# A fixed order for the ELU steps, weight casts, x operands and output copies between the first and the second chunk of an attention and feed-forward kernel

## The chip, the cores and the metric

The kernel runs on one core of a Trainium2 chip. Its time is that of one execution on the device, in microseconds (us), and the figure of a kernel is the median of its runs. A profile is one more execution, recorded by the hardware profiler; positions in it are us from the start of its span. PE is TensorE's matmul, DVE is VectorE, ACT is ScalarE, POOL is GpSimd, SP is the queue that issues the transfers.

## The reference

Attention over 8 sequences of 576 tokens with 8 heads of 64 is followed by a feed-forward block with an ELU; both in float32. Four heads see a window of 32 keys, four see every fourth key of a window of 128:

```python
scores = scale * np.matmul(q, k.transpose(0, 1, 3, 2))
scores = np.where(masks[None, :, :, :], scores, -1000000000.0)
attn = np.exp(scores - np.max(scores, axis=-1, keepdims=True))
attn = attn / (np.sum(attn, axis=-1, keepdims=True) + 1e-09)
x = np.matmul(attn, v)            # then [B, S, H * D] as 4608 rows of 512
h = x @ w_in                      # 512 -> 2048
g = np.where(h > 0.0, h, np.exp(np.minimum(h, 0.0)) - 1.0)
return g @ w_out                  # 2048 -> 512
```

## The kernel before, in words

**Chunks and tiles.** The feed-forward block goes over nine chunks of 512 tokens (`c`), and in a chunk over 16 tiles of 128 hidden features (`f`). Tile `f` of chunk `c` is `gemm1(c, f)`: `x` times a block of `w_in`, into one bank of PSUM, `h0` or `h1`. In chunk 0 the banks alternate; from chunk 1 on the tiles all use `h0`, and `h1` is lent to the attention. Then come the ELU steps, and two tiles later (`LAG = 2`, kept by the list `pend` and by `flush`) `second_product`: four groups of three matmuls that add the tile's share to the output banks `o_ps`. "Tile 14's product" below is this second product of `f = 14` in chunk 0.

**Split operands.** A matmul in full precision is made of three: every operand is cast to a high part (ACT, `copy` into a rounded type) and a rest (DVE, `tensor_tensor` subtract). `split_w` (lines 180 and 181) makes both for two blocks of 128x512 weights at once: `split_w(15, ...)` makes those of the second products of tiles 14 and 15, and `split_late(0)` those of the first products of tiles 0 and 1, used from chunk 1 on (in chunk 0 these tiles went in full precision). `split_late(0)` writes to the room `r3`, which held raw words of weights until their conversion (lines 137 to 149, DVE). `split_x(c)` (lines 521 and 522) makes `xh` and `xl` of the chunk's `x` for four pairs of heads; chunk 1 takes 64 tokens of sequence 0 and 448 of sequence 1, so it is 8 casts on ACT and 8 rests on DVE. There is one buffer for each of `xh` and `xl`, so they can be written only when the last tile of the chunk before has read them. The first product of a tile is 12 matmuls: for each pair of heads the high weights by `xh` and by `xl`, then the rest of the weights by the four `xh`.

**ELU steps of a tile** (`elu`): exp (line 550) and relu (552) on ACT, `max(h, 0) - e` on DVE (557), the cast `gh` on ACT (563) and the rest `gl` on DVE (564). The DVE step at line 557 is the last reader of the PSUM bank in chunk 0. In chunk 1, ACT first copies the bank to SBUF (548), and lines 559 and 560 stand for relu and the DVE step.

**Attention beside it.** While chunk 0 runs, `second_attention` makes `x` of sequence 1, one step for each tile: scores (E), probabilities with six transposes on DVE at line 405 (X), outputs (O) for four pairs of heads. The X step of the last pair is at `f = 12`, O of the third pair at `f = 14` and O of the last at `f = 15`. An O step is products on PE into `a_ps` and two copies on ACT (line 286 or 289) into `x32`, from which `split_x(1)` reads. At the first tile of chunk 1 a piece of scores for sequence 2 follows tile 14's product; it uses both `a_ps` banks and `h1`.

**What sets the order.** PE's instructions stay in the order in which they are written (`mm` marks each with `inorder`). On the other engines a planner orders the instructions by a simulated time line and the order of writing; `tc.issue_after(ins)` adds that what follows on the engine of `ins` comes behind it, and `inorder` (`keep_in_program_order`) pins an instruction behind the one written just before it on its engine. `vec` and `act` (lines 412 to 420) are DVE and ACT with every instruction pinned so; before, they are used in the last tiles of chunk 2 and in the chunks from 3 on. Each engine's queue runs in order, so an instruction that waits holds all behind it.

At the border the kernel before has these lines:

```python
        if c == 1:
            with tc.issue_after(hidden[-4]), tc.issue_after(below[-4]):
                last_x = split_x(c)
...
            while c == 1 and split < min(12, f + 2):
                with tc.issue_after(last_transpose[1] if split < 2 else last_x[0]), tc.issue_after(low[NF - 3 - F2] if split < 2 else last_x[1]):
                    with tc.issue_after(low[-1]), tc.issue_after(high[-1]):
                        split_late(split)
```

so `split_late(0)` is behind `gh` and `gl` of tile 15.

Of the kernel before, what the change touches and what calls it, by code (L numbers as in the profile page):

```python
# [66 lines left out]
def body(ctx: ExitStack, tc: tile.TileContext, q, k, v, masks, w_in, w_out, out):  # L67
# [105 lines left out]
        o = k % 2 * 2  # L173
        return slots(f"r{1 + (k - 12) // 2}", o, o + 4), slots(f"r{1 + (k - 12) // 2}", o + 1, o + 5)

    def split_w(k, t0, t1, places=None):

        h, l = places or places_of(k, t0, t1)
        w = full2[k][:, t0:t1, :]
        nc.scalar.copy(out=h, in_=w)  # L180
        nc.vector.tensor_tensor(out=l, in0=w, in1=h.bitcast(F32), op=ALU.subtract)
        for t in range(t0, t1):
            wh[need[2 * k + t]], wl[need[2 * k + t]] = h[:, t - t0, :], l[:, t - t0, :]

    LATE = {0: (("r3", 0, 1), ("r3", 2, 3)), 1: (("r3", 4, 5), ("r3", 6, 7)), 2: (("a7", 0, 1), ("a7", 2, 3)),
# [107 lines left out]
    def outputs(b, hp, places, vt, tr, keep=lambda ins: ins):  # L293
        products(places, vt, tr)
        return copies(b, hp, places, keep)
# [10 lines left out]
    def banks():  # L306

        return [ps_a.tile([P, TC], F32, name=f"a_ps{i}") for i in range(2)]
# [199 lines left out]

    masked, maxima = [], []

    def split_x(c):
        for hp in range(NC):
            xh[hp] = xp.tile([P, TC], F32R, name=f"xh{hp}")
            xl[hp] = xp.tile([P, TC], F32R, name=f"xl{hp}")
            t0 = c * TC
            while t0 < (c + 1) * TC:
                b, o = divmod(t0, S)
                n = min(S - o, (c + 1) * TC - t0)
                u = slice(t0 - c * TC, t0 - c * TC + n)
                src = x32[b][:, hp, o:o + n]  # L520
                last_cast = nc.scalar.copy(out=xh[hp][:, u], in_=src)
                last = nc.vector.tensor_tensor(out=xl[hp][:, u], in0=src, in1=xh[hp][:, u].bitcast(F32), op=ALU.subtract)
                t0 += n
        return last.ins, last_cast.ins

# [13 lines left out]
    def gemm1(c, f):  # L539
        for h_ps in first if (c, f) == (0, 0) else product1(c, f):  # L540
            pass
        return h_ps

    def elu(h_ps, c, f, v=nc.vector, a=nc.scalar):
        e = fp.tile([P, TC], F32, name="e")
        if 0 < c < B - 1:
            h = fp.tile([P, TC], F32, name="h", bufs=2)
            a.copy(out=h, in_=h_ps)
            h_ps = h
        a.activation(out=e, in_=h_ps, func=AF.Exp)  # L550
        if c == 0:
            below.append(nc.scalar.activation(out=e, in_=e, func=AF.Relu, scale=-1.0, bias=1.0).ins)
            if f < F2:
                g = fp.tile([P, TC], F32, name="gh", bufs=3)
                hidden.append(nc.vector.scalar_tensor_tensor(out=g, in0=h_ps, scalar=0.0, in1=e, op0=ALU.max, op1=ALU.subtract).ins)
                return g, None
            hidden.append(nc.vector.scalar_tensor_tensor(out=e, in0=h_ps, scalar=0.0, in1=e, op0=ALU.max, op1=ALU.subtract).ins)
        else:
            a.activation(out=e, in_=e, func=AF.Relu, scale=-1.0, bias=1.0)
            v.scalar_tensor_tensor(out=e, in0=h_ps, scalar=0.0, in1=e, op0=ALU.max, op1=ALU.subtract)  # L560
        gh = slots("r3", 4)[:, 0, :] if (c, f) == (CS - 1, NF - 1) else fp.tile([P, TC], F32R, name="gh", bufs=3)
        gl = slots("r3", 6)[:, 0, :] if (c, f) == (CS - 1, NF - 2) else slots("a7", 0)[:, 0, :] if (c, f) == (CS - 1, NF - 1) else fp.tile([P, TC], F32R, name="gl", bufs=2)
        high.append(a.copy(out=gh, in_=e).ins)
        low.append(v.tensor_tensor(out=gl, in0=e, in1=gh.bitcast(F32), op=ALU.subtract).ins)
        return gh, gl

    def store(c, t, o_ps):
        o = fp.tile([P, DM], F32, name="e")
# [189 lines left out]
    def second_attention():  # L758

        x32[1] = xp.tile([P, NPAIR, S], F32, name="x32", bufs=2)  # L760
        state = [None] * NPAIR

        for step in " E0 X0 E1 X1 O0  E2 X2 O1  E3 X3  O2 O3".split(" "):
            if step:
                what, hp = step[0], int(step[1])
                i = NPAIR + hp
                if what == "E":
                    s_ps = banks()
                    scores(s_ps, *qk_of.pop(i), True)
                    state[hp] = exponentials(1, hp, [[(0, NU, a)] for a in s_ps])  # L770
                    load_qk(i + 1)
                    if hp == 0:
                        load_v(i + 1)
                    if hp == NPAIR - 1:
                        load_qk(i + 2)
                elif what == "X":
                    state[hp] = probabilities(*state[hp])
                else:
                    b, _, tr = state[hp]
                    outputs(b, hp, [(a, i * NA, (i + 1) * NA) for i, a in enumerate(banks())], v_of.pop(NPAIR + hp), tr)  # L780
                    load_v(i + 2)
            yield

    rooms = [room(0, hp) for hp in range(NPAIR)]

# [36 lines left out]
    split = 0  # L822
    pend = []
    made = {}

    def flush(n):
        while len(pend) > n:
# [4 lines left out]
    att = second_attention()  # L832
    for c in range(CS):
        if c == 1:
            with tc.issue_after(hidden[-4]), tc.issue_after(below[-4]):
                last_x = split_x(c)

        elif c > 1:
            split_x(c)
        if c == 1:  # L840
            for j in (14, 15, 12, 13, *range(12)):
                keep_whole(j)
        when = WHEN.get(c, ())
        for f in range(NF):
            while c == 0 and ready < min(NF, f + AHEAD):
                for j in (ready, ready + 1):
                    with tc.issue_after(below[-1] if below else last_copy.ins):
                        magnitude(j)
                if f > 0:
                    with tc.issue_after(last_conversion.ins):  # L850
                        last_conversion = convert(ready // 2, behind=maxima[-1] if maxima else None)
                for j in (ready, ready + 1):
                    if j + 2 * NR < NF:
                        load_w(j + 2 * NR)
                ready += 2
            if c == 0 and f == F1 - 2:
                with tc.issue_after(masked[-1]), tc.issue_after(below[-1]):
                    split_x(0)
# [3 lines that stand above are left out]
                        split_late(split)  # L862
                split += 1
            strict = (vec, act) if c == CS - 1 and f >= LAST else ()
            pend.append((c, f, elu(gemm1(c, f), c, f, *strict)))
            if c == 1:
                keep_plain(f)
            if (c, f) == (0, 0):

                for part in slice(0, 2 * DM), slice(2 * DM, 4 * DM):  # L870
                    with tc.issue_after(last_conversion.ins), tc.issue_after(hidden[-1]):
                        last_conversion = convert(1, part=part)
            if c == 0 and F1 <= f + 2 <= NF:

                with tc.issue_after(hidden[-2]):
                    split_w(f + 1, 0, 2 if f >= F2 else 1)
            if c == 0:
                with tc.issue_after(hidden[-1] if f > 1 else last_step[NPAIR - 1]):
                    next(att)
            flush(LAG if c < CS - 1 or f < NF - 2 else LAG + f - (NF - 3))  # L880
            if (c, f) in COMBINE:
                with tc.issue_after(low[-1]), tc.issue_after(high[-1]):
                    combine(COMBINE[c, f])
            if (c, f) == (CS - 1, NF - 2):
                made[0] = scores_piece(CS + 1, (0, 1))
            if f in when:
                i = when.index(f)
                if i % 2 == 0:
                    made[i] = scores_piece(c + 1, (i, i + 1))
                else:  # L890
                    outputs_piece(made.pop(i - 1))
            if (c, f) == (CS - 1, OPER):
                take_places()
                moving["temporary"], late = [halved(slots("a5", o)) for o in range(2)], moving["temporary"]
                for what in sum(OPERANDS[:7], []):
                    moving_operand(CS, what, vec, act)
# [73 lines left out]
```

## Time and profile before

| | |
|---|---|
| median of 3 runs | 894.13 us (890.94 to 895.24) |
| the profiled execution | 892.59 us, its span 890.7 us |
| mean granted clock of TensorE | 0.990 |
| PE busy | 866.9 us, 97% |
| DVE busy | 610.1 us, 68% |
| ACT busy | 458.6 us, 51% |
| POOL busy | 6.0 us, 1% |
| DMA | 170.68 MB, mean 192 GB/s |

The span is from the first to the last recorded instruction; the profiled execution's time has 1.9 us more around it. A row of a time line gives the start, the time from the first start to the last end of the instructions merged in it, engine, line, operation, output and inputs by the program's names, and in square brackets the idle time of the engine before it and what ended that. Matmuls overlap, so the time from one start to the next is what one costs. PEclk is the clock that the throttle granted to TensorE, as a share of the full one.

### The profile page before, as it was taken

How to read it: one execution, taken by the hardware profiler on the slowest of the kernel's cores; microseconds unless marked ns; L12 is line 12 of the kernel's file. 1: busy time of each engine (PE TensorE's matmuls, PEld its weight loads, DVE VectorE, ACT ScalarE, POOL GpSimd, SP SyncE). 2: the span in 40 equal slices, each digit the busy share in tenths (PEclk: the TensorE clock that was granted, in tenths of full speed). 3: DMA queues.
4: the chain of work that ended last, by engine and by line, in shares of the span. 5: the costliest groups of instructions: out<-in, count | busy, mean ns of one | idle time of the engine just before them, and what ended most of it. 6: DMA issues, size and time to landing. Idle time of an engine off the chain costs nothing. (4 is left out here: it accounts for less than half of the span.)

```text
span 890.7 us, 17847 instructions
## 1 busy us (share of the span) xinstructions
PE 866.9 (97%) x7424; PEld 728.4 (82%) x7424; DVE 610.1 (68%) x921; ACT 458.6 (51%) x783; POOL 6.0 (1%) x12
## 2 busy tenths in 40 slices
PE   6999998999989999999999999999999999999998
PEld 4545676887878888898989998989899999998996
DVE  6999996958578878874977487748775533353332
ACT  3665665745655564544554454545554453454334
POOL 2000000000000000000000000000000000000000
PEclk8999998999999999999999999999999999999999
DMA  9996334321463556867576577666765566567541
GB/s 345 380 353 244 118 102 142 109 91 67 160 223 114 192 176 197 255 191 222 179 252 212 182 221 226 220 199 221 212 186 160 175 206 186 171 182 221 185 142 48
DMA packets 66961, 170.68 MB, mean 192 GB/s; under 512 B 6752, under 2 KB 21440, under 8 KB 66880
## 3 DMA queue, kind: packets, MB, share of 16 engines
q1 hardware_dynamic: 66880, 169.54, 59.2%
q8 instruction: 59, 0.97, 0.4%
q14 instruction: 22, 0.18, 0.1%
HBM read 141.20 MB, written 28.31 MB: 190 GB/s over the span
## 5 line engine op out<-in xcount | busy, mean ns | idle before, releaser
L104 PE MATMUL h<-xh,r 128*128 128x256 f32 (+1 forms) x984 | 225.3, 311 | 8.3 <-ACT r L180 3.7
L104 PEld LDWEIGHTS h<-xh,r 128*128 128x128 f32 x984 | 166.2, 192 | 19.9 <-ACT r L180 4.2
L104 PE MATMUL h<-xl,r 128*128 128x256 f32 (+1 forms) x492 | 143.6, 309 | 0.6 <-DVE xl L418 0.6
L104 PE MATMUL o_ps<-a,r 128*128 128x512 f32 x480 | 117.0, 391 | 0.0
L418 DVE SCALAR_TENSOR_TENSOR a-1_3251<-a-1_3251,a 128x1024 f32<-128x1024 f32 x48 | 58.7, 1223 | 83.2 <-ACT a L418 83.0
L418 DVE TENSOR_TENSOR a-1_3251<-h,e 128x512 f32<-128x512 f32 x72 | 49.7, 690 | 82.5 <-PE h L104 82.1
L104 PEld LDWEIGHTS h<-xl,r 128*128 128x128 f32 x492 | 94.4, 192 | 10.4 <-issue 3.5
L104 PEld LDWEIGHTS o_ps<-a,r 128*128 128x128 f32 x480 | 87.6, 188 | 16.5
L104 PE MATMUL o_ps<-a,gh 128*128 128x512 f32 x248 | 89.3, 463 | 0.0
L418 ACT COPY e<-h 128x512 f32<-128x512 f32 x72 | 42.2, 586 | 79.2 <-PE h L104 64.8
L104 PE MATMUL h<-a,r 128*128 128x256 f32 x576 | 77.5, 284 | 0.0
L104 PEld LDWEIGHTS h<-a,r 128*128 128x128 f32 x576 | 74.0, 191 | 3.0
L418 ACT COPY a-1_3251<-h 128x512 f32<-128x512 f32 x24 | 14.1, 587 | 109.6 <-PE h L104 109.6
L104 PEld LDWEIGHTS o_ps<-a,gh 128*128 128x128 f32 x248 | 46.3, 188 | 24.2 <-issue 17.2
L418 ACT ACTIVATE a<-a 128x1024 f32<-128x1024 f32 (+1 forms) x56 | 57.0, 1030 | 1.3
L104 PE MATMUL o_ps<-r,r 128*128 128x512 f32 x212 | 56.8, 391 | 0.0
L104 PE MATMUL o_ps<-a,a 128*128 128x512 f32 x216 | 54.6, 391 | 0.0
L418 ACT ACTIVATE a<-a-1_3251 128x1024 f32<-128x1024 f32 x48 | 51.0, 1062 | 1.3 <-DVE a-1_3251 L418 0.5
L104 PEld LDWEIGHTS o_ps<-a,a 128*128 128x128 f32 x216 | 39.4, 189 | 7.4
L418 ACT CAST r<-a-1_3251 128x1024 fp32r<-128x1024 f32 x32 | 33.6, 1051 | 22.2 <-DVE a-1_3251 L418 22.1
L104 PEld LDWEIGHTS o_ps<-r,r 128*128 128x128 f32 x212 | 38.7, 188 | 7.3
L418 DVE TENSOR_TENSOR r<-a-1_3251,r 128x1024 fp32r<-128x1024 f32 x32 | 39.0, 1218 | 6.6 <-ACT r L418 6.1
(176 smaller groups left out, 1434.0 us busy)
## 6 DMA issues: line engine op xcount, KB each, us to landing
r<-combined SPq DMA_DIRECT2D x168, 512.0 KB, 4.1
vt<-v SPq DMA_DIRECT2D x30, 384.0 KB, 4.3
kt<-k SPq DMA_DIRECT2D x30, 304.0 KB, 4.6
out<-e SPq DMA_DIRECT2D x35, 256.0 KB, 3.3
qt<-q SPq DMA_DIRECT2D x30, 288.0 KB, 3.9
r<-w_in SPq DMA_DIRECT2D x16, 512.0 KB, 7.8
r<-w_out SPq DMA_DIRECT2D x16, 512.0 KB, 7.9
combined<-a SPq DMA_DIRECT2D x20, 256.0 KB, 3.4
```

What stands on the lines that cost most here:

```text
L104: return inorder(nc.tensor.matmul(*args, **kw))
L418: return lambda *args, **kw: inorder(getattr(self.eng, name)(*args, **kw))
```

## The change

From tile 14 of chunk 0 to the first tile of chunk 1, the steps on ACT and DVE are written out in the order in which they are to be issued, with `vec` and `act`:

- `elu` is cut into three steps (`elu_steps`: exp and relu; the DVE step; `gh` and `gl`), `split_w` into two (`split_steps`: the cast; the rest).
- At tile 14: exp and relu of tile 14; behind the O step's copies the cast of `split_late(0)`.
- At tile 15: the rest of `split_late(0)`, then tile 14's DVE step. The last O step makes its products here, its two copies are left for later.
- Ahead of chunk 1: the x operands of two pairs of heads, the last O step's copies, the x operands of the other two pairs, `gh` and `gl` of tile 14, the cast and rest of `split_w(15)` (before, written at tile 14), then exp, relu, the DVE step, `gh` and `gl` of tile 15. `split` starts at 1, since `split_late(0)` is done.
- The two `issue_after` around `split_x(1)` are gone. What `flush` lets wait is lowered by one or two at tiles 14 and 15, which are appended to `pend` only later, so PE's order stays as it was.

No instruction and no transfer is added or taken away.

```diff
-    def split_w(k, t0, t1, places=None):
+    def split_steps(k, t0, t1, places=None, v=nc.vector, a=nc.scalar):
         h, l = places or places_of(k, t0, t1)
         w = full2[k][:, t0:t1, :]
-        nc.scalar.copy(out=h, in_=w)
-        nc.vector.tensor_tensor(out=l, in0=w, in1=h.bitcast(F32), op=ALU.subtract)
+        a.copy(out=h, in_=w)
+        yield
+        v.tensor_tensor(out=l, in0=w, in1=h.bitcast(F32), op=ALU.subtract)
...
-    def split_x(c):
+    def split_x(c, v=nc.vector, a=nc.scalar, between=None):
         for hp in range(NC):
+            if between is not None and hp == NC - 2:
+                between()
...
+    def elu_steps(h_ps):
+        e = fp.tile([P, TC], F32, name="e")
+        act.activation(out=e, in_=h_ps, func=AF.Exp)
+        below.append(act.activation(out=e, in_=e, func=AF.Relu, scale=-1.0, bias=1.0).ins)
+        yield
+        hidden.append(vec.scalar_tensor_tensor(out=e, in0=h_ps, scalar=0.0, in1=e, op0=ALU.max, op1=ALU.subtract).ins)
+        yield
+        gh, gl = fp.tile([P, TC], F32R, name="gh", bufs=3), fp.tile([P, TC], F32R, name="gl", bufs=2)
+        high.append(act.copy(out=gh, in_=e).ins)
+        low.append(vec.tensor_tensor(out=gl, in0=e, in1=gh.bitcast(F32), op=ALU.subtract).ins)
+        yield gh, gl
...
@@ second_attention, an O step
-                    outputs(b, hp, [(a, i * NA, (i + 1) * NA) for i, a in enumerate(banks())], v_of.pop(NPAIR + hp), tr)
+                    places = [(a, i * NA, (i + 1) * NA) for i, a in enumerate(banks())]
+                    products(places, v_of.pop(NPAIR + hp), tr)
+                    if hp < NPAIR - 1:
+                        copies(b, hp, places)
+                    else:
+                        state[hp] = b, hp, places
                     load_v(i + 2)
-            yield
+            yield state[-1]
...
         if c == 1:
-            with tc.issue_after(hidden[-4]), tc.issue_after(below[-4]):
-                last_x = split_x(c)
+            last_x = split_x(c, vec, act, lambda: copies(*last_outputs, inorder))
+            pend.append((0, NF - 2, next(ends[0])))
+            split_w(NF - 1, 0, 2, None, vec, act)
+            next(ends[1])
+            next(ends[1])
+            pend.append((0, NF - 1, next(ends[1])))
+            split = 1
...
-            pend.append((c, f, elu(gemm1(c, f), c, f, *strict)))
+            if c == 0 and f >= NF - 2:
+                ends.append(elu_steps(gemm1(c, f)))
+                if f == NF - 2:
+                    next(ends[0])
+                    first_late = split_steps(0, 0, 2, [slots(*a) for a in LATE[0]], vec, act)
+                else:
+                    for _ in first_late:
+                        pass
+                    next(ends[0])
+            else:
+                pend.append((c, f, elu(gemm1(c, f), c, f, *strict)))
...
-            if c == 0 and F1 <= f + 2 <= NF:
+            if c == 0 and F1 <= f + 2 < NF:
                 with tc.issue_after(hidden[-2]):
                     split_w(f + 1, 0, 2 if f >= F2 else 1)
             if c == 0:
                 with tc.issue_after(hidden[-1] if f > 1 else last_step[NPAIR - 1]):
-                    next(att)
-            flush(LAG if c < CS - 1 or f < NF - 2 else LAG + f - (NF - 3))
+                    last_outputs = next(att)
+                if f == NF - 2:
+                    next(first_late)
+            flush(LAG - 1 - (f == NF - 1) if c == 0 and f >= NF - 2 else LAG if c < CS - 1 or f < NF - 2 else LAG + f - (NF - 3))
```

More of the change, by code (lines that the diff above doesn't have):

```diff
@@ L174, in places_of, with split_w @@
         return slots(f"r{1 + (k - 12) // 2}", o, o + 4), slots(f"r{1 + (k - 12) // 2}", o + 1, o + 5)
-    def split_w(k, t0, t1, places=None):
+    def split_steps(k, t0, t1, places=None, v=nc.vector, a=nc.scalar):
         h, l = places or places_of(k, t0, t1)
         w = full2[k][:, t0:t1, :]
-        nc.scalar.copy(out=h, in_=w)
-        nc.vector.tensor_tensor(out=l, in0=w, in1=h.bitcast(F32), op=ALU.subtract)
+        a.copy(out=h, in_=w)
+        yield
+        v.tensor_tensor(out=l, in0=w, in1=h.bitcast(F32), op=ALU.subtract)
         for t in range(t0, t1):
             wh[need[2 * k + t]], wl[need[2 * k + t]] = h[:, t - t0, :], l[:, t - t0, :]
+    def split_w(*args):
+        for _ in split_steps(*args):
+            pass
     LATE = {0: (("r3", 0, 1), ("r3", 2, 3)), 1: (("r3", 4, 5), ("r3", 6, 7)), 2: (("a7", 0, 1), ("a7", 2, 3)),
@@ L520, in split_x @@
                 src = x32[b][:, hp, o:o + n]
-                last_cast = nc.scalar.copy(out=xh[hp][:, u], in_=src)
-                last = nc.vector.tensor_tensor(out=xl[hp][:, u], in0=src, in1=xh[hp][:, u].bitcast(F32), op=ALU.subtract)
+                last_cast = a.copy(out=xh[hp][:, u], in_=src)
+                last = v.tensor_tensor(out=xl[hp][:, u], in0=src, in1=xh[hp][:, u].bitcast(F32), op=ALU.subtract)
                 t0 += n
@@ L824, in body @@
     made = {}
+    ends = []
     def flush(n):
@@ L864, in body @@
             strict = (vec, act) if c == CS - 1 and f >= LAST else ()
-            pend.append((c, f, elu(gemm1(c, f), c, f, *strict)))
+            if c == 0 and f >= NF - 2:
[5 more added lines that the diff above has]
+                    for _ in first_late:
+                        pass
+                    next(ends[0])
+            else:
+                pend.append((c, f, elu(gemm1(c, f), c, f, *strict)))
             if c == 1:
```

## The prediction

> **What bounds the kernel now.** First the cores' view and the page's first part, for the span and the busiest engine:
>
> ```profile
> core 0: 890.7 us, clock 0.990
> ```
> ```profile
> PE 866.9 (97%) x7424; PEld 728.4 (82%) x7424; DVE 610.1 (68%) x921; ACT 458.6 (51%) x783; POOL 6.0 (1%) x12
> ```
>
> PE is busy for 97%, in the order written, so the time moves only where PE waits or where its clock is low. Next I listed PE's own waits by stretch of the run. From 145 us to the end there are these five groups (us in total, times, longest):
>
> ```profile
> PE h L104 <- issue: 2.4, 1, 2.4
> PE h L104 <- ACT h L548: 1.0, 1, 1.0
> PE h L104 <- PE h L104: 1.0, 1, 1.0
> PE h L104 <- ACT nothing L475: 0.8, 3, 0.3
> PE h L104 <- DVE xl L418: 0.6, 1, 0.6
> ```
>
> That is 5.8 us in 745. The longest single wait behind the start-up lies at the border of chunks 0 and 1, where the change is. PE's time line there:
>
> ```profile
> 128.73 0.39 PE L104 MATMUL h<-xh,r 128*128 128x512 f32 x1
> ...
> 130.55 1.07 PE L104 MATMUL h<-xh,r 128*128 128x512 f32 x4
> 131.54 1.21 PE L104 MATMUL a_ps<-pt,vt 128*64 128x96 f32 x24
> 132.69 0.74 PE L104 MATMUL o_ps<-r,gh 128*128 128x512 f32 x2
> ...
> 135.35 0.39 PE L104 MATMUL o_ps<-r,gl 128*128 128x512 f32 x1
> 139.49 0.80 PE L104 MATMUL h<-xh,r 128*128 128x512 f32 x1 [3.75 <-ACT r L180]
> ...
> 144.78 0.90 PE L104 MATMUL o_ps<-r,gh 128*128 128x512 f32 x2
> ```
>
> Tile 15's first product begins at 128.73, the last O step's products at 131.54, tile 13's product at 132.69. Then PE stands until the cast of `split_late(0)` (line 180) lets chunk 1 begin at 139.49. The table by stretches (length, busy us of PE, PEld, DVE, ACT, POOL, then the clock) shows a second loss behind it:
>
> ```profile
> 135.60:139.50 3.90, 0.15 (x2) 0.01 (x1) 2.74 (x7) 3.60 (x9) 0.00 (x0) 0.88 0.00 0
> 139.50:145.50 6.00, 6.00 (x14) 4.71 (x15) 2.33 (x2) 1.37 (x2) 0.00 (x0) 0.51 0.66 219
> 150.00:175.00 25.00, 25.00 (x116) 20.73 (x111) 23.71 (x39) 16.55 (x27) 0.00 (x0) 1.00 0.45 154
> ```
>
> For 6.0 us behind the wait the clock is 0.51. What is late is seen on ACT and DVE:
>
> ```profile
> 127.90 0.39 ACT L286 COPY x<-a_ps 128x288 f32<-128x288 f32 x1
> 132.90 0.62 ACT L563 CAST gh<-e 128x512 fp32r<-128x512 f32 x1 [4.61 <-DVE e L557]
> 133.43 1.94 ACT L521 CAST xh<-x 128x64 fp32r<-128x64 f32 x6
> 135.27 0.58 ACT L550 ACTIVATE e<-h 128x512 f32<-128x512 f32 x1
> 135.76 0.23 ACT L521 CAST xh<-x 128x64 fp32r<-128x64 f32 x1
> 135.89 0.69 ACT L286 COPY x<-a_ps 128x288 f32<-128x288 f32 x2
> 136.47 0.64 ACT L552 ACTIVATE e<-e 128x512 f32<-128x512 f32 x1
> 137.00 0.56 ACT L521 CAST xh<-x 128x448 fp32r<-128x448 f32 x1
> 137.87 0.62 ACT L563 CAST gh<-e 128x512 fp32r<-128x512 f32 x1 [0.30 <-DVE e L557]
> 138.40 1.99 ACT L180 CAST r<-a 128x1024 fp32r<-128x1024 f32 x2
> ```
> ```profile
> 126.94 3.47 DVE L405 STREAM_TRANSPOSE pt<-sm 32x384 f32<-32x384 f32 x6
> 130.44 1.23 DVE L181 TENSOR_TENSOR r<-a,r 128x1024 fp32r<-128x1024 f32 x1
> 131.58 0.68 DVE L564 TENSOR_TENSOR gl<-e,gh 128x512 fp32r<-128x512 f32 x1
> 132.19 0.68 DVE L557 SCALAR_TENSOR_TENSOR e<-h,e 128x512 f32<-128x512 f32 x1
> 133.55 0.69 DVE L564 TENSOR_TENSOR gl<-e,gh 128x512 fp32r<-128x512 f32 x1 [0.69 <-ACT gh L563]
> 134.16 2.23 DVE L522 TENSOR_TENSOR xl<-x,xh 128x64 fp32r<-128x64 f32 x7
> ...
> 146.96 0.69 DVE L560 SCALAR_TENSOR_TENSOR e<-h,e 128x512 f32<-128x512 f32 x1 [5.13 <-ACT e L559]
> ```
>
> ACT stands for 4.61 us, since tile 14's `gh` at its queue's head waits for DVE, which is busy with transposes, the rest of `split_w(15)` (130.44), tile 13's `gl` and tile 14's step. Behind the head stand the x casts, tile 15's steps and, last, the cast that PE needs.
>
> **The change part by part.** Prices are from one start to the next in these rows: a weight cast 0.95 (two in 1.99), its rest 1.14 (130.44 to 131.58), `gl` 0.61, the DVE step 0.60, `gh` 0.53 (132.90 to 133.43), exp 0.58, relu 0.64, the two copies 0.58 (135.89 to 136.47), the x casts of a pair 0.61 (135.27 less 133.43, for three), its rests 0.70 (2.23 for seven of eight).
>
> *Cast of `split_late(0)`, moved ahead.* Pinned behind the copies at 127.90 it runs about 128.3 to 129.3, inside the 4.61 us in which ACT stood, and so costs nothing. Its room `r3` is free: the conversion that read it is ahead of the transposes on DVE.
>
> *Rest of `split_late(0)`, moved ahead, and `split_w(15)`, moved back.* On DVE one 1.14 takes the other's place: transposes to 130.44, tile 13's `gl` to 131.05, the rest to 132.19, tile 14's step to 132.8, where it ended before. On ACT the cast for tile 15 leaves the stretch ahead of 126. Tile 13's product at 132.69 finds its `gl` as before.
>
> *x operands.* The casts no longer stand behind tile 14's `gh`, but need tile 15's first product to have read `xh`: for the first pair that is its ninth matmul, at 130.55 plus 0.39, so about 131.0. Two pairs on ACT: 131.0 to 132.2. Then the copies wait for the last O step's products (131.54 plus 1.21): 132.8 to 133.4; then the other pairs to 134.6. On DVE the rests begin behind tile 14's step: 132.8 to 134.2, the other two to 135.6.
>
> *PE.* Tile 13's product ends at 135.35 plus one matmul. Eight matmuls take 130.55 less 128.73, which is 0.2275 each, so chunk 1 can begin at 135.58. The first `xl` is there at 133.5 and the last at 135.6, needed by the eighth matmul at 137.2: slack 2 and 1.6 us.
>
> *Added waits.* Tile 14's `gh` and `gl` now stand behind all x operands: 134.6 to 135.2 and to 136.2. The cast of `split_w(15)` follows to 136.2, its rest on DVE to 137.4. Tile 14's product begins at 135.58 plus twelve matmuls, 138.3, and its second matmul needs that rest: slack 1.1 us, the smallest. Tile 15's exp and relu go to 137.4, its DVE step to 138.0, `gh` and `gl` to 139.4; the step frees `h1`, which the piece of scores needs behind tile 14's product, at 141: slack 3 us. What is queued behind these on both engines is chunk 1's own work, which needs the new matmuls anyway. SP and POOL get nothing moved past them: none of the moved steps issues a transfer.
>
> *Sum.* The start of chunk 1 moves from 139.49 to 135.58: 3.9 us. Without the wait the clock has no reason to fall: 6.0 us at 0.51 do the work of 3.06, so 2.9 us more. The twelve matmuls alone say 5.29 (144.78 less 139.49) against 2.73, 2.6 us, and tile 14's first pair the rest. Together 6.8 us of PE's path.
>
> [...]
>
> *Behind it.* Can DVE follow a PE that comes 6.8 us sooner? From 150 to 175 it is busy for 23.71 of 25 us, so there it has no reserve. But between the border and there it stood 5.13 us for tile 0 of chunk 1, and 0.69 us for `gh`, waits that went with PE's lateness: 5.8 us at hand. The missing 1 us falls on steps used two tiles later, so I charge nothing for it, with 1 us as the bound. Chunks 1 and 2 are planned anew where nothing is pinned: their waits of 5.8 us in all can vanish or grow. The bound below is the longest, 2.4 us, gone; above, one more like it. I take zero, since the work there is the same.
>
> The profiled execution took 892.59 us (span 890.7 and 1.9 around it): less 6.8 is 885.8. The median of the runs is 1.5 us higher, 894.13, and gives 887.3. I take the middle, 886.6.
>
> **The rivals.**
>
> *A part of the wait stays (889 to 891).* The smallest slack is 1.1 us, by prices that are exact to some tenths, and it rests on the transposes ending at 130.44. If the fixed chain is 3 us late, PE waits 2 us or so at tile 14's product. What that does to the clock is seen at the longest of the later waits:
>
> ```profile
> 256.69 0.40 PE L104 MATMUL h<-xh,r 128*128 128x512 f32 x1 [2.39 <-issue]
> ```
> ```profile
> 258.10:261.50 3.40, 3.40 (x10) 2.68 (x9) 2.35 (x5) 2.48 (x4) 0.00 (x0) 0.51 0.98 320
> ```
>
> A wait of 2.39 us was followed by 3.40 us at 0.51, which is 1.7 us more: 4.1 in all, so 2.7 of the 6.8 are left, about 891. At 1 to 2 us and a full clock it is 888 to 889. Against it: nothing in the chain waits for an engine that isn't on time in the rows above. [...]
>
> *The gain is given back later (890 to 893).* DVE is the engine without reserve from 150 on. If it can't follow, or if the new plan of chunks 1 and 2 brings a wait such as the one at 256 (4.1 us), some 2 to 5 us of the 6.8 remain lost. For it: the plan is free there. Against it: a `gl` is needed two tiles after its tile, and PE had no wait at all from 150 to 175 with DVE at 95%.
>
> *The chain is put ahead of the transposes (893 and more; no gain, or slower).* The pin ties the rest of `split_late(0)` only to the instruction written before it, not to the six transposes. If the planner issues that rest, tile 14's step and the rests of the first two pairs first (1.14, 0.60 and 1.40, the latter waiting for 131.0), the transposes run from about 132.6 to 136.1, the last O step's products wait on PE from 131.54 to 136.1, 4.6 us, and the clock falls behind that for 2.9 more: 7.5 lost against 6.8 won, about 893.3 on the scale of the forecast. It decides when more than about 4 us of chain stand ahead of the transposes. Against it: the transposes are written two tiles earlier, and DVE went into them without a pause.
>
> **How the numbers follow.** The wait and the slow stretch both gone, 0.62 (884 to 889). A part of the wait stays, 0.16. Given back later, 0.14. The chain ahead of the transposes, or a worse plan, 0.08. From one run to the next the kernel before spreads from 890.94 to 895.24, so half a per cent, 4.5 us, is what a measurement can tell; that is a time below 889.6. Faster: all of the first case and under half of the second, 0.69. Same: the rest of the second, the third and half of the last, 0.25. Slower 0.06. The range goes from 883.5 (the forecast less the later wait of 2.4 and some spread) to 893.0, which leaves out the last case and the spread of the third.
>
> **What would show it.** In the profile after: chunk 1's first matmul at about 135.6 with no wait in brackets, and a clock of 1.00 from 135 to 146; the weight cast of line 180 on ACT near 128.3, ahead of the x casts, which begin at 131; tile 14's product near 138.3, the piece of scores near 141.3; PE's sum of waits behind 145 still near 6 us and the span near 884. It is wrong if PE waits for `gl`, line 181 or `xl` at 135 to 139, if the transposes are not ended by 131, or if a new wait of over 2 us with a clock of 0.51 stands in chunks 1 or 2.

## The result, and the profile after

The median of the kernel after is 887.91 us (885.59 to 889.17), that of the kernel before beside it 893.43 us (890.94 to 895.24): a ratio of 0.9935, 95% interval 0.9918 to 0.9952. It is faster by 5.5 us, or 0.65%; the prediction said 886.6 us. The profiled execution took 886.14 us against 892.59.

The cores' view and the page's first part of the kernel after:

```profile
core 0: 884.3 us, clock 0.995
```
```profile
PE 862.6 (98%) x7424; PEld 725.1 (82%) x7424; DVE 610.2 (69%) x921; ACT 458.5 (52%) x783; POOL 6.0 (1%) x12
```

The counts of instructions are as before, and the span is 6.4 us shorter. PE's time line of the kernel after at the border of chunks 0 and 1:

```profile
129.17 0.39 PE L104 MATMUL h<-xh,r 128*128 128x512 f32 x1
...
135.79 0.39 PE L104 MATMUL o_ps<-r,gl 128*128 128x512 f32 x1
136.02 0.39 PE L104 MATMUL h<-xh,r 128*128 128x512 f32 x1
137.83 1.07 PE L104 MATMUL h<-xh,r 128*128 128x512 f32 x4
138.74 0.62 PE L104 MATMUL o_ps<-r,gh 128*128 128x512 f32 x2
...
141.23 0.39 PE L104 MATMUL o_ps<-r,gl 128*128 128x512 f32 x1
```

No row has a wait in brackets. Chunk 1's first matmul, at 136.02, follows tile 13's product without a pause, and tile 14's product begins at 138.74. For all kernels I use one measure of the border: from the start of tile 15's first product to the start of the last matmul of tile 14's product. Here it is 141.23 less 129.17, so 12.06 us. Before, it began at 128.73 and ended with this row of PE's time line:

```profile
147.57 0.39 PE L104 MATMUL o_ps<-r,gl 128*128 128x512 f32 x1
```

That was 18.84 us, so the border gave 6.78 us. From the end of the border to the end of the span it is 743.1 us in both profiles. The table by stretches of the kernel after (columns as in the prediction):

```profile
135.60:139.50 3.90, 3.90 (x19) 3.23 (x18) 3.21 (x5) 2.97 (x5) 0.00 (x0) 1.00 0.19 75
139.50:145.50 6.00, 6.00 (x164) 4.89 (x163) 4.47 (x7) 3.94 (x7) 0.00 (x0) 1.00 0.34 112
150.00:175.00 25.00, 24.11 (x107) 19.64 (x106) 22.70 (x37) 16.35 (x27) 0.00 (x0) 1.00 0.28 97
```

PE is busy for 3.90 of 3.90 us where it was busy for 0.15, and the clock is 1.00 where it was 0.51. ACT's and DVE's time lines of the kernel after (line 424 is the helper through which pinned instructions go):

```profile
127.43 0.40 ACT L292 COPY x<-a_ps 128x288 f32<-128x288 f32 x1
127.71 1.07 ACT L424 CAST r<-a 128x1024 fp32r<-128x1024 f32 x1
131.41 1.33 ACT L424 CAST xh<-x 128x64 fp32r<-128x64 f32 x4 [2.63 <-PE h L104]
132.75 0.90 ACT L292 COPY x<-a_ps 128x288 f32<-128x288 f32 x2
133.54 1.33 ACT L424 CAST xh<-x 128x64 fp32r<-128x64 f32 x4
134.76 0.62 ACT L424 CAST gh<-e 128x512 fp32r<-128x512 f32 x1
```
```profile
127.41 0.68 DVE L572 TENSOR_TENSOR gl<-e,gh 128x512 fp32r<-128x512 f32 x1
128.01 3.47 DVE L411 STREAM_TRANSPOSE pt<-sm 32x384 f32<-32x384 f32 x6
131.52 1.23 DVE L424 TENSOR_TENSOR r<-a,r 128x1024 fp32r<-128x1024 f32 x1
132.66 0.69 DVE L424 SCALAR_TENSOR_TENSOR e<-h,e 128x512 f32<-128x512 f32 x1
133.26 2.76 DVE L424 TENSOR_TENSOR xl<-x,xh 128x64 fp32r<-128x64 f32 x8
135.94 0.68 DVE L424 TENSOR_TENSOR gl<-e,gh 128x512 fp32r<-128x512 f32 x1
136.54 1.22 DVE L424 TENSOR_TENSOR r<-a,r 128x1024 fp32r<-128x1024 f32 x1
```

The cast that was last on ACT, at 138.40, stands at 127.71 in time that had been idle. What ACT still waits for in front of the x casts is PE's reading of `xh`, not DVE.

PE's waits of the kernel after from 145 us on (us in total, times, longest):

```profile
PE h L104 <- ACT h L556: 2.3, 3, 1.0
PE h L104 <- issue: 2.1, 1, 2.1
PE h L104 <- PE h L104: 1.0, 1, 1.0
PE h L104 <- ACT nothing L481: 0.7, 2, 0.5
PE h L104 <- DVE xl L424: 0.6, 1, 0.6
```

With 0.3 us more in one smaller wait that is 7.0 us, against 5.8 before. But before, the stop marked "issue" was followed by 1.7 us lost to a slow clock, and in this profile it isn't.

### The profile page after: what moved, and what is told of

It reads as the page before. It is cut to its first block, busy times and chain, and to the rows that moved or that the text cites. A ratio compares the mean times of both kernels' runs of the same rounds, so it can differ in the third digit from the quotient of the medians.

```text
span 884.3 us, 17848 instructions
## 1 busy us (share of the span) xinstructions
PE 862.6 (98%) x7424; PEld 725.1 (82%) x7424; DVE 610.2 (69%) x921; ACT 458.5 (52%) x783; POOL 6.0 (1%) x12
```

## The experiments

The times are medians. Ratios are to the kernel before on the same chip, with 95% intervals. "Border" is the measure above, from the one profile of each kernel.

| kernel | border, us | us | ratio |
|---|---|---|---|
| before | 18.84 | 893.43 | 1 |
| the change | 12.06 | 887.91 | 0.9935 [0.9918, 0.9952] |
| warm | 16.11 | 893.42 | 1.0003 [0.9992, 1.0015] |
| late_cast | 17.46 | 892.60 | 0.9989 [0.9977, 1.0001] |
| cast_only | 14.67 | 888.56 | 0.9946 [0.9930, 0.9961] |
| no_pins | 14.63 | 890.83 | 0.9970 [0.9956, 0.9983] |
| after_again | 12.06 | 888.47 | 0.9936 [0.9921, 0.9950] |
| early15 | 12.06 | 888.81 | 0.9936 [0.9920, 0.9952] |
| slack1 | 12.30 | 889.64 | 0.9948 [0.9933, 0.9962] |
| slack3 | 14.82 | 889.96 | 0.9952 [0.9940, 0.9965] |
| warm_same_plan | 16.59 | 888.95 | 0.9950 [0.9934, 0.9967] |
| shift40 | 12.06 | 886.27 | 0.9928 [0.9909, 0.9947] |
| shift44 | 12.06 | 884.48 | 0.9904 [0.9882, 0.9925] |
| shift56 | 12.06 | 886.33 | 0.9932 [0.9907, 0.9956] |

**warm: the wait stays, the clock doesn't fall.** The kernel before, with 17 matmuls into the bank of chunk 1's first tile, ahead of that tile. They fill the wait, and the tile overwrites what they make.

```diff
+        if (c, f) == (1, 0):
+            for _ in range(17):
+                mm(h_ps, wh[30][:, :P], wh[30], start=True, stop=True)
```

> The kernel before, with 17 extra matmuls of 128x512 (operands of tile 15's weights, ready long before) into the bank h0 ahead of chunk 1's first product, which then overwrites them. They fill the 3.9 us in which PE stood. Theory (the sum has two terms, the wait of 3.9 us and the slow clock behind it of 2.9 us): the real product starts at about 139.5 as before, the clock stays at 1.00 from 139.5 to 145.5, and the time falls by 2.9 us against the kernel before. Rival (the clock falls for another reason, such as the transfers of that stretch, and not for PE's idleness): the clock is 0.51 there as before and the time is the same. Rival (the gain is of the order, not of the clock): same time.

PE's time line and the table by stretches of this kernel:

```profile
136.12 4.01 PE L104 MATMUL h<-r 128*128 128x512 f32 x17
140.03 0.50 PE L104 MATMUL h<-xh,r 128*128 128x512 f32 x1
```
```profile
139.50:145.50 6.00, 6.00 (x27) 4.62 (x25) 3.08 (x4) 3.28 (x5) 0.00 (x0) 1.00 0.66 219
```

Chunk 1 starts no earlier than before, but the clock is 1.00, and the border is 2.73 us shorter: the clock's share of the 6.78. The time of the whole kernel didn't follow: its ratio is 1.0003. The matmuls had moved the planner's simulated time line, and its orders on ACT and DVE in chunks 1 and 2 came out otherwise. From the border's end to the end of the span it is 746.5 us, 3.4 more than before. Two of PE's waits of this kernel from 145 us on show where:

```profile
PE h L104 <- ACT h L551: 4.0, 3, 1.9
PE o_ps L104 <- ACT e L576: 1.6, 1, 1.6
```

**late_cast: everything but the early cast.** The kernel after, with the cast and rest of `split_late(0)` behind tile 15's last `gl`, the place they had before. The x operands keep their new order.

```diff
-                    first_late = split_steps(0, 0, 2, [slots(*a) for a in LATE[0]], vec, act)
...
+            split_w(0, 0, 2, [slots(*a) for a in LATE[0]], vec, act)
             split = 1
```

> The changed kernel, with both steps of split_late(0) put back behind gh and gl of tile 15 (still in a fixed order). Theory (the early cast is what the wait hung on; x operands ahead of gh gain nothing without it): x operands are ready by 135 but the cast ends near 139.6, PE waits about 3.8 us for it, the clock falls to 0.51 for 6 us, and the time is that of the kernel before within 1 us. Rival (the x operands being ahead of tile 14's gh are the larger part): the wait shrinks by 2 us or more, 3 to 5 us faster than before.

PE's time line and the table by stretches of this kernel:

```profile
139.71 0.79 PE L104 MATMUL h<-xh,r 128*128 128x512 f32 x1 [3.68 <-ACT r L424]
```
```profile
139.50:145.50 6.00, 5.79 (x19) 4.70 (x20) 2.36 (x2) 2.38 (x5) 0.00 (x0) 0.73 0.66 219
```

The wait is back, 3.68 us for the cast of the weights, and the time with it. So the order of the x operands alone brings nothing: the cast was what PE waited for. The clock is worth a look: 0.73 over 6.0 us is 1.6 us, of which 1.5 fall behind the wait, not 2.9. After nearly the same wait the slow stretch was half as long. In finer steps of the trace the clock is at 0.5 from 139.32 to 142.73 here, which is 3.41 us, and from 138.53 to 145.36 before, which is 6.83 us and begins while PE still waits. So the 6.0 us of the row before were no fixed length.

**cast_only: the early cast and nothing else.** The kernel before, with `split_late(0)` behind tile 14's O step, unpinned.

```diff
             if c == 0:
                 ...
                     next(att)
+                if f == NF - 2:
+                    split_late(0)
+                    split = 1
```

> The kernel before, with split_late(0) written at tile 14 behind the O step, and nothing else of the change: no pins, x operands behind tile 14's gh as before, split_w(15) at its old place. On DVE the plan puts its rest ahead of tile 13's gl, so all that follows there is 1.14 us later than before. Theory (both are needed: the cast early, and the x operands not behind gh): PE starts chunk 1 near 135.7, but the last pair's xh and xl come near 138.7 and 139.5, so its first product ends 2.3 us late in two or three short waits; the clock stays up or falls briefly; 3 to 4.5 us faster than before, 2 to 4 us slower than the change. Rival (the cast alone suffices): 6 to 7 us faster, as the change.

PE's time line of this kernel:

```profile
138.35 0.49 PE L104 MATMUL h<-xh,r 128*128 128x512 f32 x1 [0.81 <-ACT xh L521]
139.16 0.50 PE L104 MATMUL h<-xl,r 128*128 128x512 f32 x1 [0.31 <-DVE xl L522]
```

PE now waits for x operands, which still stand behind tile 14's `gh`. The border is 4.17 us shorter, of the change's 6.78. The rest is what the fixed order of the x operands adds: 2.6 us here. In the times the two can't be told apart: the intervals of their ratios overlap (medians 888.56 and 887.91), so most of what the whole kernel gains comes with the early cast alone.

**no_pins: the change's order of writing, without pins.** The kernel after, with `nc.vector` and `nc.scalar` in place of `vec` and `act` in the new steps, and the copies unpinned.

```diff
-            last_x = split_x(c, vec, act, lambda: copies(*last_outputs, inorder))
+            last_x = split_x(c, nc.vector, nc.scalar, lambda: copies(*last_outputs))
...
-            split_w(NF - 1, 0, 2, None, vec, act)
+            split_w(NF - 1, 0, 2)
```

> The changed kernel with everything written in the same order, but on the plain engines, without pins. The planner puts tile 14's gh ahead of all x casts again, lets the cast of split_w(15) run ahead of tile 13's gh and its rest behind that of split_late(0), as in the kernel with the cast alone. Theory (the pins do the work of putting x operands ahead of gh): as the kernel with the cast alone, 3 to 4.5 us faster than before, first product of chunk 1 ends 2.3 us late. Rival (the order of writing is enough): 6 to 7 us faster, as the change.

PE's time line of this kernel, and a stretch of chunk 2:

```profile
139.67 0.49 PE L104 MATMUL h<-xh,r 128*128 128x512 f32 x1 [0.81 <-ACT xh L529]
```
```profile
250.00:262.00 12.00, 8.87 (x45) 6.83 (x35) 8.82 (x17) 5.24 (x9) 0.00 (x0) 0.72 0.82 282
```

The planner puts tile 14's `gh` ahead of all x casts again, as in cast_only, and the border is the same to 0.04 us. So it is the pins and not the order of writing that bring the last 2.6 us at the border. The median is 2.3 us above cast_only's. Both profiles have a stop of 3.1 us in chunk 2, to which I come below; here a slow clock comes with it (0.72 in this stretch), in cast_only's none does.

**early15: `split_w(15)` back at tile 14.** The kernel after, with that one move undone.

```diff
-            split_w(NF - 1, 0, 2, None, vec, act)
...
-            if c == 0 and F1 <= f + 2 < NF:
+            if c == 0 and F1 <= f + 2 <= NF:
```

> The changed kernel with split_w(15) written at tile 14 as in the kernel before, the rest of the fixed order kept. DVE has 1.14 us more ahead of the x operands. Theory (there was slack of 1.6 us at the last xl): the first xl come about 1.1 us later, the last at about 137.0 against a need at 137.6, no wait on PE, the same time as the change within 1 us; moving split_w(15) back was not needed. Rival (DVE is so full that 1.14 us come through to PE): 1 us slower than the change, or 2.5 with a fall of the clock.

The border is 12.06 us and the ratio 0.9936, as with the change: this move wasn't needed. On DVE, the x rests of this kernel begin here:

```profile
133.69 2.77 DVE L424 TENSOR_TENSOR xl<-x,xh 128x64 fp32r<-128x64 f32 x8
```

Tile 15's first product began at 128.50, so that is 5.19 us behind it, against 4.09 (133.26 less 129.17) with the change: one weight rest later, and PE doesn't wait for it.

**after_again, slack1 and slack3: how much room the chain has.** after_again is the kernel after once more. The other two repeat the rest of `split_w(15)` on DVE, once or three times, so that tile 14's product gets it later.

```diff
             split_w(NF - 1, 0, 2, None, vec, act)
+            h, l = places_of(NF - 1, 0, 2)
+            for _ in range(1):                    # slack3: range(3)
+                vec.tensor_tensor(out=l, in0=full2[NF - 1][:, 0:2, :], in1=h.bitcast(F32), op=ALU.subtract)
```

> The changed kernel as it is, on the chip of the next three, to compare them with: 5.5 to 6.5 us faster than the kernel before.

> The changed kernel with the rest of split_w(15) computed twice (the same values again): 1.14 us more on DVE, at the place with the smallest slack of the prediction, ahead of tile 14's product. Theory (slack about 1.1 us there, and DVE can take 1 us behind it): PE waits 0 to 0.2 us at tile 14's product, time within 1 us of the change. Rival (DVE has no reserve behind the border): 1.1 us slower.

> The changed kernel with the rest of split_w(15) computed four times: 3.4 us more on DVE. Theory: PE waits 3.4 less 1.1, about 2.2 us, at tile 14's product; a wait of that length lets the clock fall (as after the 2.39 us wait at 256 of the kernel before), so 2.2 to 3.9 us slower than the change, at most 1 us more downstream. [...] Rival (DVE has no reserve downstream): 3.4 us slower or more, in later waits for gl.

PE's time line of slack3, and its stretch behind it:

```profile
141.15 0.50 PE L104 MATMUL o_ps<-r,gh 128*128 128x512 f32 x1 [2.43 <-DVE r L424]
```
```profile
139.50:145.50 6.00, 4.35 (x155) 3.52 (x155) 5.61 (x8) 4.00 (x7) 0.00 (x0) 1.00 0.15 47
```

One more rest (about 1.2 us) costs the border 0.24 us, and no row shows a wait; three (3.7 us) cost 2.76 and a wait of 2.43 us. So the room at tile 14's product is about 1 us, as worked out in the prediction (1.1). The clock stays at 1.00 behind 2.43 us. In the medians slack3 is 1.5 us above after_again, less than the 2.76 at the border, and slack1 1.2 us above, more than its 0.24: their plans of chunks 1 and 2 aren't those of the change.

**warm_same_plan: the clock's share with the old plan.** As warm, with 20 matmuls. The built kernel then has DVE's order of the kernel before and ACT's but for one instruction.

```diff
-            for _ in range(17):
+            for _ in range(20):
```

> The kernel before, with 20 instead of 17 extra matmuls ahead of chunk 1's first product, so that the planner's order on DVE is that of the kernel before to the last instruction and on ACT but for one. Theory (with 17 the 2.7 us won at the border were lost to a worse order that the planner made for chunks 1 and 2): the real product starts about 0.6 us late, the clock stays up, and now the time is 2 us below that of the kernel before. Rival (what is won in clock at the border is lost anyway, since DVE and ACT cannot follow): the same time as before, with new waits for ACT's copies of h behind the border.

The border is 2.25 us shorter with this table by stretches:

```profile
139.50:145.50 6.00, 6.00 (x28) 4.99 (x27) 2.67 (x3) 2.97 (x5) 0.00 (x0) 1.00 0.66 219
```

Chunk 1 starts 0.6 us later than before, since the 20 matmuls outlast the wait, so the clock's share is 2.9 us, near warm's 2.73. The median is 5.0 us lower, more than the profiles account for: 2.25 us at the border and 1.1 behind it (742.0 us from there, before 743.1), where the stop in chunk 2 is absent. The remaining 1.7 us aren't explained. Between 17 and 20 matmuls lie 4.5 us, nearly the effect of the change, and in the profiles the stretch behind the border differs by as much (746.5 and 742.0).

**shift40, shift44, shift56: PE's instructions moved by some places.** The profiles have one stop of PE in common, at 249 to 257 us behind the same matmul of a tile of chunk 2, marked "issue": 2.4 us before, 2.1 with the change, 3.5 in after_again. To tell a stop that hangs on the place of PE's instructions from one that hangs on the tile's data, the kernels here are the change with N tiny matmuls (8 columns) in `first_attention`, over 100 us ahead of it; their output is overwritten.

```diff
+        if hp == 0:
+            for _ in range(N):                    # 40, 44 and 56
+                mm(s_ps[:8, 0, :8], ones_sb[:, :8], mask_sb[:, 0, :8], start=True, stop=True)
```

> As the last, with 40 tiny matmuls, so 80 places; the order on ACT and DVE again that of the changed kernel. [...] Rival as above.

> As the last, with 44 tiny matmuls: 8 places more, but the planner makes another order in chunk 2 (on ACT an exp of the attention and a gh cast change places with others, on DVE some 15 instructions). Theory (orders that the planner makes behind the border cost or win 1 to 3 us, whatever the change is): differs from the kernel with 40 by 1 us or more, in waits for ACT or DVE between 250 and 300. Rival (these orders are worth nothing measurable): the same within 0.7 us.

> The changed kernel with 56 tiny matmuls (8 by 8, overwritten) ahead of the first scores, where PE waits 2.35 us for the first k. The order on ACT and DVE is that of the changed kernel to the last instruction; PE's instructions all stand 112 places later. In every run so far PE stopped behind the sixth matmul of the same tile of chunk 2 at about 250, with no releaser shown, for 1.7 to 3.5 us, mostly with a clock of 0.51 behind it; only where 17 matmuls more stood ahead of it did it not stop there. [...] Rival (the wait hangs on data of that tile): it stays at the seventh matmul with 2 us or more, and the time is that of the change.

PE's time line at that place: the change, the same kernel again, then shift44:

```profile
248.97 0.39 PE L104 MATMUL h<-xl,r 128*128 128x512 f32 x1
251.47 0.39 PE L104 MATMUL h<-xh,r 128*128 128x512 f32 x1 [2.11 <-issue]
```
```profile
249.32 0.39 PE L104 MATMUL h<-xl,r 128*128 128x512 f32 x1
253.24 0.39 PE L104 MATMUL h<-xh,r 128*128 128x512 f32 x1 [3.52 <-issue]
```
```profile
247.63 0.39 PE L104 MATMUL h<-xl,r 128*128 128x512 f32 x1
247.86 0.39 PE L104 MATMUL h<-xh,r 128*128 128x512 f32 x1
```

And the table by stretches of the three, in the same order:

```profile
250.00:262.00 12.00, 10.53 (x47) 8.72 (x47) 11.19 (x20) 6.41 (x11) 0.00 (x0) 1.00 0.69 232
```
```profile
250.00:262.00 12.00, 8.77 (x32) 7.04 (x32) 9.06 (x17) 5.04 (x9) 0.00 (x0) 0.86 0.70 233
```
```profile
250.00:262.00 12.00, 11.96 (x53) 9.58 (x52) 11.40 (x23) 7.25 (x13) 0.00 (x0) 1.00 0.76 250
```

The stop is gone in all three, and in warm and warm_same_plan, which also shift what comes later on PE. shift40 and shift56 have the orders of ACT and DVE that the change has, so the stop hangs on the place of PE's instructions and not on data. shift40 and shift56 are 1.6 us below the change's median, measured at another time and with intervals that overlap, so that gain isn't shown. Other stops marked "issue" appear elsewhere (1.0 and 1.1 us in shift40, 0.7 and 1.1 in shift44, 2.8 in shift56). shift44 is the fastest of all kernels here: its runs (883.65 to 884.81) lie below every run of the change (885.59 to 889.17) and of after_again (886.75 to 890.53). Against shift40 it has some instructions of chunk 2 in another order on ACT and DVE, and the expectation put a difference down to that. The medians differ by 1.8 us, but the profiles don't show the planner's order as the cause: shift44's span is 2.5 us shorter, of which 2.2 lie ahead of tile 15's first product (at 129.15 for 131.38) and 0.3 behind the border (741.8 for 742.1).

## Why the prediction was right

*The start of chunk 1.* The step said that chunk 1 begins 6.85 us behind tile 15's first product (135.58 less 128.73). Measured: 6.85 (136.02 less 129.17). The prices from one start to the next held, and so did the chain: the cast in ACT's idle time, x casts from about 131, copies, x casts, `gh`.

*Tile 14's product.* Predicted 9.57 us behind the same start, measured 9.57. The smallest slack was put at 1.1 us; the rest of `split_w(15)` ends at 137.76 and is needed by the second matmul at about 138.97, so it was 1.2, and slack1 and slack3 bracket it.

*The sum.* 6.8 us predicted, 6.78 at the border. The 18.84 us are of the profile from which the sum was made, so what this tests is the 12.06 us: that PE then runs without a wait and at full clock. The sum's two terms come apart on the chip. The clock term is shown by warm (2.73) and warm_same_plan (2.9), against 2.9. The wait term hangs on the cast (late_cast: wait back; cast_only: 4.17 of 6.78 without any pin), and the pins bring the last 2.6 there (no_pins).

*What the sum missed.* The medians fell by 5.5 us, and by 5.0 in after_again, not by 6.8. One part is visible: the second term was sized from a single profile of before. Behind nearly the same wait late_cast lost 1.5 us to the clock, not 2.9. If runs of the kernel before fall between the two, the term is worth 1.5 to 2.9 and the sum 5.4 to 6.8. The slow stretch of the profile before was 6.83 us long, of which the prediction's row showed 6.0, and late_cast's was 3.41. What sets the length isn't shown, nor whether this is the whole of the missing 1.3 us. That 886.6 is also 893.43 less 6.8 is luck: the forecast took the middle between two starting points, and the kernel before came out 0.7 us lower beside the change than its median of three runs.

*Behind the border.* The term of zero came out as zero in the profiles (743.1 us each), but not because nothing changed: waits for ACT's copies of `h` grew from 1.0 to 2.3 us, and the slow clock behind the stop was absent. after_again, with the same instructions, needs 747.2 us from the border on. The bound given there, the later stop gone or one more like it, was of the right kind and size: in the two profiles of one kernel the stretch from 250 to 262 alone has PE busy for 10.53 and 8.77 us.

*The rivals.* "A part of the wait stays" did not come: no wait stands at 135 to 139. Its price was wrong for this place: it took from the 2.39 us row that the clock falls behind such a wait, and behind slack3's 2.43 us it didn't. Nor does the wait's length alone decide it in these profiles: behind the stop in chunk 2 a slow clock followed 2.4 us in late_cast (0.86 from 250 to 262), and none followed 3.1 us in cast_only (1.00 there). A wait of 2 to 3.5 us is thus a chance of a fall here, not a fall. "Given back later" did not come with the change, but did in full in warm. "The chain ahead of the transposes": in the profile the transposes come first (128.01, the rest of `split_late(0)` at 131.52). They ended 1.0 us later than predicted (131.48 for 130.44): 0.44 is tile 15's later start, 0.6 that the planner put tile 13's `gl` in front of them instead of behind. For the chain behind them that is the same sum, and the last O step's products on PE, at 131.98, still found them done. That rival's order was not tried.

## What to carry to other kernels

When the bottleneck engine waits for one late instruction, look on that instruction's engine for time that stood idle behind a queue's head: moving the one cast there won 4.2 us at the border, and fixing the order of its neighbours 2.6 more there, which the medians can't tell from nothing. Price a wait on TensorE with the clock behind it, but as a range (from nothing behind slack3's 2.43 us to 2.9 behind the 3.75 us of before), and from more than one profile. Where a planner orders the rest, compare the built orders before an edit is credited or blamed: three more filler matmuls moved the time by 4.5 us. And look in the profiles where a difference lies: that of shift40 and shift44 lay for the most part ahead of everything that had been reordered.

## What the runs showed of the hardware that was not expected

The stop marked "issue" in chunk 2 came in every kernel whose PE instructions stood at the old places, behind the same matmul, for 1.7 (early15) to 3.5 us, and in none whose instructions had moved by 34 to 112 places. What ends it isn't shown, but a transfer lies beside it. The pages of before and after both have this row of a queue of the kind "instruction" (packets, MB, share of the DMA engines):

```profile
q8 instruction: 59, 0.97, 0.4%
```

Those are 59 packets of 16 KB. In both profiles one of them lands shortly before PE goes on: before at 255.16 for 256.69, with the change at 250.11 for 251.47. It started 0.02 us before the stop of 2.39 us, and 0.13 us before the one of 2.11. Two packets that lie alike beside two stops don't show that PE waits for them.

What sets the time of the packet is open too. With the change the stop, from 249.36, comes behind many small matmuls (146 in the table's row from 246 to 248, 13 in that from 244 to 246) and beside busy transfers (a DMA share of 0.88 from 246 to 248). But the packet took 0.88 us at both stops, as short as any of the other 58, which took 0.88 to 1.71 us before and to 2.03 with the change. No run took the transfers away.

In the same built kernel the stop was 2.1 us with a full clock behind it in one execution, and 3.5 us with a clock of 0.86 over 12 us in another: 1.4 and 1.7, so 3.1 of the 4.5 us between the two profiles' spans. In this pair it makes most of the difference; how much it makes of the spread over all runs isn't shown.

The slow clock, too, came in two lengths: 3.41 us (before at 258.00, late_cast at the border) and 6.83 (before at the border). For the stop in chunk 2 the length can be estimated from the tables by stretches, with a slow clock of 0.50: 3.4 us in late_cast and after_again (0.86 over 12 us), 6.7 to 6.9 in no_pins and slack1 (0.72 over 12 us) and in slack3 (0.50 and 0.65 over 4 us each). What sets these lengths isn't shown. A wait behind which the clock fell cost about 1.7 or 3.4 us here, half of such a stretch, less the part of it that passed while PE still waited.
